# The first half of kv in neighbouring PSUM places, and x of two pairs in separate PSUM tiles

## The chip, the cores and the metric

The kernel runs on one core of one Trainium2 chip. The metric is the device time of one execution in microseconds (us); for one kernel I quote the median of its runs, with lowest and highest. All runs in this document were in the fast state, with a granted TensorE clock between 0.998 and 1.0 in the profiled ones. "The trace" is the record of one profiled execution, and its times count from the start of that execution's span. In the lines of the profile PE is TensorE at its matmuls, PEld TensorE loading weights, DVE VectorE, ACT ScalarE and POOL GpSimd; "issue" is time in which an engine waited for nothing that the profile shows. The chain is the work that ended last, followed back from the end. PSUM is the memory into which the matmuls write; it comes in banks, and a tile is a buffer that the kernel asks for, here of one or two banks.

## The reference

Linear attention over 8 batches of 8 heads (576 positions, 64 wide), followed by a two-layer feed-forward net with exact GELU over all 4608 tokens:

```
q_s = softmax of q over the head's 64 entries
k_s = softmax of k over the 576 positions
kv  = einsum('bhsd,bhse->bhde', k_s, v)        # 64 x 64 a head
x   = einsum('bhsd,bhde->bhse', q_s, kv)       # -> 4608 x 512, heads side by side
h   = x @ w_in                                 # 512 -> 2048
out = gelu(h) @ w_out                          # 2048 -> 512
```

The output is fp32. The kernel multiplies in bf16.

## The kernel before

Heads are taken two at a time, so a batch has four pairs (hp 0 to 3). For each batch the kernel makes kv of the pairs on TensorE (`kv_mm`, in two halves of two pairs), divides by the softmax sum of k on VectorE (`kv_norm`, result `kvc` in bf16), makes x from q and kvc (`x_mm`), copies x out of PSUM (`x_evac`, on VectorE with "v" or ScalarE with "s"), and then runs the two large products (`h_phase`, `y_phase`) on 512 tokens. The parts that matter here, with cuts:

```python
def kv_mm(b, half):
    if "kv" not in st[b]:
        st[b]["kv"] = psum_a.tile([128, 2, 2, 256], FP32, tag="a2", name="kv")   # two banks
    ps = st[b]["kv"]
    for n in range(NS):
        for i in range(2):                      # pair 2*half + i; i chooses the bank
            for hh in range(2):
                ...
                nc.tensor.matmul(ps[c, i, half, 0:D + 1], ek[...], v_aug[...],
                                 start=(n == 0), stop=(n == NS - 1))

def kv_norm(b, h0, h1):
    ps = st[b]["kv"]
    nc.vector.reciprocal(rec[:, :, 0:m], ps[:, :, h0:h1, D])
    nc.vector.tensor_tensor(out=kvc[b]..., in0=ps[:, :, h0:h1, 0:D], in1=rec..., op=ALU.mult)

# batch 0
kv_mm(0, 0)
kv_norm(0, 0, 1)
warm_x()                                        # four matmuls on zeros, to fill the wait
kv_mm(0, 1)
kv_norm(0, 1, 2)
x_mm(0, 0)
...
# batch 1, in between the second product of batch 0
xx = psum_a.tile([128, 2, M], FP32, tag="a2", name="xx")       # one tile, two banks
st[1]["x2"], st[1]["x3"] = xx[:, 0], xx[:, 1]
x_mm(1, 1)                                      # x of pairs 2 and 3
x_evac(1, 2)                                    # VectorE
x_evac(1, 3, "s")                               # ACT
...
h_phase(1, ..., groups={0: 2})                  # the first two column groups take turns
```

The softmax here doesn't subtract the row's maximum and nothing guards it: scores larger than these inputs give would overflow.

## Time and profile before

| | before |
|---|---|
| median of the first 3 runs | 279.95 us (279.80 to 280.01) |
| span of the profiled run | 278.2 us |
| TensorE (PE) busy | 271.6 us, 98% |
| large matmuls: pace in a full stage | 64 in 13.81 us, 0.2158 us each |
| stop in batch 0, before the second half of kv | 0.40 us |
| step from the sixth to the seventh matmul of batch 1's first product | 0.392 us (0.216 elsewhere) |

The page's shares are averages; that TensorE is the bound follows from the chain, where it makes 95% of what ended last. The last two rows of the table are the two holes in TensorE's stream that the change aims at. The lines that carry them stand in the prediction below.

### The profile page before, as it was taken

The page shows a single profiled execution, that of the slowest core. Times are in us where ns is not written, and L with a number is a line of the kernel's source. Part 1 is how long each engine was busy: PE and PEld are TensorE (multiplying, and loading weights), DVE is VectorE, ACT ScalarE, POOL GpSimd, SP SyncE. Part 2 cuts the span into 40 slices and gives each one's busy share as a digit, 9 for nine tenths or more (in the row PEclk, how much of TensorE's full clock was granted, in tenths as well). Part 3 has the DMA queues.
Part 4 walks back from the last instruction along what each step waited for, and adds up shares of the span by engine and source line. Part 5 has one row for each costly group of instructions (what it writes and reads, how often), then busy time and mean ns, then how long its engine had stood idle before and what let it go on. Part 6 is the DMA issues. An engine that isn't in the chain of part 4 may idle for free.

```text
span 278.2 us, 4570 instructions
## 1 busy us (share of the span) xinstructions
PE 271.6 (98%) x1924; PEld 126.0 (45%) x1924; DVE 100.7 (36%) x151; ACT 158.5 (57%) x246; POOL 33.9 (12%) x25
## 2 busy tenths in 40 slices
PE   7799999999999999999999999999999999999994
PEld 3344454444444444444444444444444444444443
DVE  2876574309743540183008400651015200120012
ACT  4867666689377816791569246943683363126400
POOL 1630050002020220014000500050005000000000
PEclk9999999999999999999999999999999999999999
DMA  7999999963993149602981199117401500220033
GB/s 255 396 394 431 398 398 407 400 247 94 292 350 62 65 106 282 268 38 85 268 329 38 43 229 390 50 48 192 112 0 75 151 2 0 75 78 0 0 78 77
DMA packets 44980, 50.10 MB, mean 180 GB/s; under 512 B 20384, under 2 KB 29856, under 8 KB 44704
## 3 DMA queue, kind: packets, MB, share of 16 engines
q1 hardware_dynamic: 44560, 49.39, 53.1%
q10 hardware_dynamic: 400, 0.43, 0.5%
q8 instruction: 15, 0.25, 0.4%
q14 instruction: 5, 0.04, 0.1%
HBM read 36.70 MB, written 9.44 MB: 166 GB/s over the span
## 4 chain that ended last, share of the span: by engine, by line
PE 95%; DMA 2%; DVE 1%; POOL 1%; ACT 0%; issue 0%; POOLq 0%
PE ps L311 44%; PE ps L321 44%; PE kv L180 2%; DMA f<-in_q_dram 2%; PE ps L268 1%; PE ps L346 1%; POOL e L212 1%; PE pair L311 1%; PE ps L229 1%; ACT e L145 0%; DVE qsum L210 0%; PE ps L273 0%; DVE kvc L191 0%; PE tp L229 0%; PE ps L430 0%
## 5 line engine op out<-in xcount | busy, mean ns | idle before, releaser
L311 PE MATMUL ps<-xT,wi_bf 128*128 128x512 bf16 x568 | 124.9, 379 | 0.0
L321 PE MATMUL ps<-wo_bf,g 128*128 128x512 bf16 x560 | 124.2, 379 | 0.0
L316 ACT ACTIVATE g<-ps 128x512 bf16<-128x512 f32 x142 | 83.8, 598 | 66.9 <-PE ps L311 66.9
L311 PEld LDWEIGHTS <-wi_bf 128*128 128x128 bf16 x576 | 56.2, 98 | 68.1 <-issue 0.7
L321 PEld LDWEIGHTS <-g 128*128 128x128 bf16 x560 | 53.9, 98 | 64.3 <-issue 0.4
L329 DVE COPY y_sb<-ps 128x512 f32<-128x512 f32 x34 | 23.2, 686 | 81.0 <-PE ps L321 80.7
L212 POOL TENSOR_TENSOR e<-e,recq 128x2048 bf16<-128x2048 bf16 (+1 forms) x9 | 25.7, 2855 | 176.4 <-DVE recq L211 148.3
L162 DVE CAST v_aug<-f 128x576 bf16<-128x576 f32 x25 | 17.1, 745 | 47.5 <-DMA f<-in_v_dram 47.5
L210 DVE TENSOR_REDUCE qsum<-e 128x16 f32<-128x1024 bf16 (+1 forms) x13 | 21.0, 1619 | 14.4 <-ACT e L145 14.4
L294 ACT CAST xT<-ps 128x512 bf16<-128x512 f32 x18 | 9.8, 589 | 25.8 <-PE ps L268 16.3
L145 ACT ACTIVATE e<-f 128x512 bf16<-128x512 f32 (+1 forms) x42 | 20.5, 556 | 3.4 <-DMA f<-in_q_dram 3.3
L150 ACT ACTIVATE ek<-f 128x2304 bf16<-128x2304 f32 (+1 forms) x10 | 17.2, 1728 | 0.5 <-DMA f<-in_k_dram 0.4
L292 DVE CAST xT<-ps 128x512 bf16<-128x512 f32 x16 | 10.3, 686 | 17.0 <-PE ps L268 14.1
L79 ACT ACT_TABLE_LOAD x9 | 11.5, 1283 | 2.8 <-issue 2.6
L430 PE MATMUL ps<-zeros 128*128 128x512 f32 (+1 forms) x16 | 8.5, 680 | 1.5 <-DVE zeros L464 1.5
L145 ACT ACT_TABLE_LOAD x7 | 9.0, 1283 | 0.1
L397 DVE CAST wi_bf<-w 128x512 bf16<-128x512 f32 x12 | 7.2, 632 | 2.3 <-DMA w<-in_moe_w_in_dram 2.0
L180 PEld LDWEIGHTS <-ek 64*64 64x64 bf16 x576 | 6.4, 105 | 2.7 <-issue 1.1
L180 PE MATMUL kv<-v_aug,ek 64*64 64x65 bf16 x576 | 6.8, 193 | 0.4 <-DVE kvc L191 0.4
L212 DVE TENSOR_TENSOR e<-e,recq 128x1024 bf16<-128x1024 bf16 x4 | 6.4, 1594 | 0.1
L423 DVE CAST wo_bf<-w 128x2048 bf16<-128x2048 f32 (+1 forms) x4 | 4.4, 1094 | 3.9 <-DMA w<-in_moe_w_out_dram 3.8
L430 PEld LDWEIGHTS ps<-zeros 128*128 128x128 f32 x14 | 3.2, 239 | 5.3 <-issue 3.8
(40 smaller groups left out, 51.2 us busy)
## 6 DMA issues: line engine op xcount, KB each, us to landing
out_dram<-y_sb SPq DMA_DIRECT2D x32, 256.0 KB, 2.4
f<-in_k_dram SPq DMA_DIRECT2D x6, 1152.0 KB, 9.5
f<-in_v_dram SPq DMA_DIRECT2D x6, 1152.0 KB, 11.6
f<-in_q_dram SPq DMA_DIRECT2D x6, 1024.0 KB, 7.2
w<-in_moe_w_in_dram SPq DMA_DIRECT2D x6, 512.0 KB, 8.8
f<-in_v_dram SPq DMA_DIRECT2D x8, 288.0 KB, 6.8
f<-in_q_dram SPq DMA_DIRECT2D x4, 512.0 KB, 8.9
w<-in_moe_w_out_dram SPq DMA_DIRECT2D x2, 1024.0 KB, 12.2
```

The lines of the kernel that those rows point to most:

```text
L79: nc.scalar.activation(out=scr[:, 1:2], in_=scr[:, 0:1], func=func)
L145: nc.scalar.activation(out=dst[:, i], in_=src[:, u], func=AF.Exp)
L150: nc.scalar.activation(out=ek[b % 2][:, i:i + n], in_=st[b]["kf"][:, i:i + n].rearrange("p x (n d) -> p x n d", n=NS), func=AF.Exp,)
L162: eng.tensor_copy(out=o, in_=i)
L180: nc.tensor.matmul(ps[c, i, half, 0:D + 1], ek[b % 2][pr, hp, n, :], v_aug[b % 2][pr, hp, n, 0:D + 1], start=(n == 0), stop=(n == NS - 1),)
L210: nc.vector.reduce_sum(out=qsum, in_=eq[:, :, hs, :], axis=AX.X)
L212: eng.tensor_tensor(out=eq[:, :, hs, :], in0=eq[:, :, hs, :], in1=recq.unsqueeze(3).to_broadcast([128, J, w, D]), op=ALU.mult,)
L311: nc.tensor.matmul(ps, wi_bf[:, dm, t * 128:(t + 1) * 128], xT[:, dm, :], start=(dm == 0), stop=(dm == NDM - 1),)
L316: nc.scalar.activation(out=g[:, t, :], in_=ps, func=AF.Gelu)
L321: nc.tensor.matmul(ps, st[c]["g"][:, t, j * 128:(j + 1) * 128], wo_bf[:, t, :], start=(t == 0), stop=(t == NDF - 1),)
L329: nc.vector.tensor_copy(out=y_sb, in_=ps)
L430: nc.tensor.matmul(ps, z[:, 0:128], z, start=True, stop=True)
```

## The change

The intent of the first part, as I read the diff: put pairs 0 and 1 into the two neighbouring places in the middle (the end of one bank and the start of the other), pairs 2 and 3 into the outer ones, so that scaling the first half reads one run of PSUM and the second half can be written meanwhile. The intent of the second: x of batch 1's pairs 2 and 3 in two tiles, so that the two engines that copy them out have nothing in common.

```diff
+    place = [1, 2, 0, 3]
+    def kvc_of(b, hp):
+        return kvc[b][:, hp if b < 2 else place[hp], :]
...
-            st[b]["kv"] = psum_a.tile([128, 2, 2, 256], FP32, tag="a2", name="kv")
+            st[b]["kv"] = psum_a.tile([128, 4, 256], FP32, tag="a2", name="kv")
...
-                        ps[c, i, half, 0:D + 1], ek[b % 2][pr, hp, n, :],
+                        ps[c, place[hp], 0:D + 1], ek[b % 2][pr, hp, n, :],
...
+            src, dst, m = ps[:, 1:3] if half == 0 else ps[:, 0::3], kvc[b][:, 2 * half:2 * half + 2], 2
...
-    xx = psum_a.tile([128, 2, M], FP32, tag="a2", name="xx")
-    st[1]["x2"], st[1]["x3"] = xx[:, 0], xx[:, 1]
+    x_tile(1, 2, psum_a, "a")
+    st[1]["x3"] = psum_a.tile([128, 2, M], FP32, tag="a2", name="xx")[:, 0]
```

The rest of the diff makes `x_mm` and `kv_norm` follow the new places; in batches 2 to 7 both halves are scaled in one instruction, as before, and kvc now keeps the order of the places.

More of the change, by code (lines that the diff above doesn't have):

```diff
@@ L180, in kv_mm, with kv_norm @@
                     nc.tensor.matmul(
-                        ps[c, i, half, 0:D + 1], ek[b % 2][pr, hp, n, :],
+                        ps[c, place[hp], 0:D + 1], ek[b % 2][pr, hp, n, :],
                         v_aug[b % 2][pr, hp, n, 0:D + 1], start=(n == 0), stop=(n == NS - 1),
                     )
-    def kv_norm(b, h0, h1):
+    def kv_norm(b, half=None):
         ps = st[b]["kv"]
-        m = h1 - h0
-        rec = small.tile([128, 2, 2], FP32, tag="reck")
-        nc.vector.reciprocal(rec[:, :, 0:m], ps[:, :, h0:h1, D])
+        if half is None:
+            src, dst, m = ps, kvc[b], 4
+        else:
+            src, dst, m = ps[:, 1:3] if half == 0 else ps[:, 0::3], kvc[b][:, 2 * half:2 * half + 2], 2
+        rec = small.tile([128, 4], FP32, tag="reck")
+        nc.vector.reciprocal(rec[:, 0:m], src[:, :, D])
         nc.vector.tensor_tensor(
-            out=kvc[b].rearrange("p (h i) d -> p i h d", i=2)[:, :, h0:h1],
-            in0=ps[:, :, h0:h1, 0:D],
-            in1=rec[:, :, 0:m].unsqueeze(3).to_broadcast([128, 2, m, D]), op=ALU.mult,
+            out=dst, in0=src[:, :, 0:D],
+            in1=rec[:, 0:m].unsqueeze(2).to_broadcast([128, m, D]), op=ALU.mult,
         )
@@ L199, in kv_step @@
         kv_mm(b, 1)
-        kv_norm(b, 0, 2)
+        kv_norm(b)
     def norm_q(b, i=0, n=1, eng=None):
@@ L268, in x_mm @@
                         nc.tensor.matmul(
-                            ps[c, :], kvc[b][pr, hp, :], st[b]["qT"][pr, :, hp, :],
+                            ps[c, :], kvc_of(b, hp)[pr], st[b]["qT"][pr, :, hp, :],
                             start=True, stop=True,
@@ L273, in x_mm @@
                         nc.tensor.matmul(
-                            ps[c, bb * R:(bb + 1) * R], kvc[bb][pr, hp, :],
+                            ps[c, bb * R:(bb + 1) * R], kvc_of(bb, hp)[pr],
                             st[b]["qT"][pr, bb // 2, hp, bb % 2 * R:(bb % 2 + 1) * R],
@@ L488 @@
     kv_mm(0, 0)
-    kv_norm(0, 0, 1)
+    kv_norm(0, 0)
     warm_x()
     kv_mm(0, 1)
-    kv_norm(0, 1, 2)
+    kv_norm(0, 1)
     x_mm(0, 0)
@@ L549 @@
     kv_mm(1, 0)
-    kv_norm(1, 0, 1)
+    kv_norm(1, 0)
     y_part(14, range(J))
@@ L557 @@
     x_evac(1, 1, "s")
-    kv_norm(1, 1, 2)
+    kv_norm(1, 1)
     y_part(15, range(J))
```

## The prediction

> **What bounds the kernel now.** I read the page first: engine shares, the 40 slices, the chain; then the chain in order of time around the two places that the diff touches (the start, batch 0, and the turn from batch 0 to batch 1), then the timeline of each engine there, then the groups by tile.
>
> ```profile
> PE 271.6 (98%) x1924; PEld 126.0 (45%) x1924; DVE 100.7 (36%) x151; ACT 158.5 (57%) x246; POOL 33.9 (12%) x25
> PE   7799999999999999999999999999999999999994
> PE 95%; DMA 2%; DVE 1%; POOL 1%; ACT 0%; issue 0%; POOLq 0%
> ```
>
> TensorE is busy in every slice, and 95% of the chain that ends last is its own work. So only what shortens TensorE's stream, or a hole in it, can move the end. Busy alone does not prove a full pace, so I checked the pace: the chain gives each full stage of the first product as 64 matmuls in 13.81 us, 0.2158 us each. The second product with its 560 and 32 matmuls (the last 32 are narrower) is at the same pace. The holes are what is left to win. The chain in order of time shows the two places:
>
> ```profile
> 12.48 0.30 DVE kvc L191
> 12.78 0.04 issue
> 12.82 0.52 PE kv L180 x35
> ```
>
> ```profile
> 44.25 0.34 PE xx L268 x4
> 44.59 1.40 PE ps L311 x6
> 45.99 0.01 issue
> 46.00 12.68 PE ps L311 x58
> ```
>
> In the first, at batch 0, TensorE stops before the second half of kv until VectorE has scaled the first half into kvc. In the second, at the start of batch 1's first product, 58 matmuls take 12.68 us, where 58 x 0.2158 = 12.52 us would do: 0.16 us is a stop before the seventh matmul. Starts of single matmuls in that trace say the same: 0.392 us between the sixth and the seventh, where 0.216 is usual, so 0.176 us lost. Between there and the tail I find no other interval of the big matmuls that is out of line; the switches to and from the 64-wide ones cost about 0.31 us each time, in every batch, and stay. What the seventh waits for is in the timeline of ACT and DVE:
>
> ```profile
> 44.64 0.69 DVE L292 CAST xT<-xx 128x512 bf16<-128x512 f32 x1 [0.20 <-PE xx L268]
> 45.37 0.59 ACT L294 CAST xT<-xx 128x512 bf16<-128x512 f32 x1 [0.82 <-DVE xT L292]
> ```
>
> The two tiles xx holds (x of pairs 2 and 3) lie in two banks and are copied out by two engines, yet ACT starts only when DVE has ended, after 0.82 us of idling. With two column groups at a time (the first group of this stage is a pair), matmuls one to six need pairs 0, 1 and 2, the seventh needs pair 3. Pair 3 is there at 45.37 + 0.586 = 45.96 and the seventh starts at 46.00.
>
> **What the Trainium skill says.** "Perfetto Trace Analysis", section "Optimization Strategy", tells to find the gaps between slices of the bounding engine and the semaphore that each waits for; that is the reading above. "TensorE: Matmul & The Clock Gate", section "Back-to-back issue gap", gives 216 ns for an isolated matmul of 512 columns (and a lower sustained figure, 131 ns, which this trace does not reach); the trace has 215.8. "PSUM — Partial Sum Buffer", section "PSUM bank collisions raise a hardware error", says that a write by TensorE and a read by another engine in one bank and quadrant collide whatever the addresses, and to guard by bank and quadrant, not by address. The trace agrees as far as it can: kv's second half waits 0.40 us for the read of the first half, at other addresses of the same banks. "VectorE: DVE Perf Modes", section "The TRN2 errata — SBUF-src ops pay a fixed extra latency per instruction", has (N+151)/0.96 ns for a fp32 tensor_tensor: 291 ns at 128 and 424 at 256. The trace has 291 for kvc at 128 and 424 to 426 at 256, in spite of its PSUM input[...].
>
> **The change part by part.** I compared the built programs: every engine has the same instructions in the same order; what differs is access patterns and a handful of waits.
>
> (1) *kv in neighbouring places.* Pairs 0 and 1 go from places 0 and 2 of 4 to places 1 and 2; pairs 2 and 3 to 0 and 3. The banks stay: places 0 and 1 are one bank, 2 and 3 the other. The aim can only be that the second half no longer falls within the span that the scaling of the first half reads, so that TensorE need not stop at 12.4 to 12.8 us. But in the changed program the first matmul of the second half has the same wait on VectorE as before, for the same count (13, the end of the scaling of the first half): the dependence is kept by bank, not by range. Removed: nothing. Of batch 1 the same: its second half comes behind x of the first half, which needs kvc anyway. Cost 0.
>
> (2) *kvc's order for batches 2 to 7.* Six scalings of 128x256 at 424 ns keep their 256 elements; by the formula above and the 424 to 426 ns of the trace they cost the same. They lie beside TensorE (DVE is 36% busy), and their result is used a stage later. Cost 0. x's matmuls read another 64-column block of kvc: same shape, 400 ns modelled, same count.
>
> (3) *x of pairs 2 and 3 in two tiles.* Pair 2 goes to the single bank "a" that held pair 0, pair 3 to the first bank of the two that held kv. The first matmul of pair 2 now waits for ACT to have emptied pair 0. That copy and the next were one 1.07 us run of ACT from 42.99, so it is done by about 43.6; x begins at 44.18. Slack 0.6 us, cost 0. The ACT copy of pair 3 now waits for TensorE (the last of the four matmuls) in place of VectorE. VectorE started on the same event at 44.64, and ACT's earlier work (y_sb, 43.95 + 0.60) ends at 44.55, so the copy starts at about 44.65 and ends at about 45.24, 0.72 us sooner. The seventh matmul, unhindered, would start at 46.00 - 0.176 = 45.83: 0.59 us after that. So the whole 0.176 us goes, and no more, since then TensorE's own pace is the limit. The fifth matmul needs pair 2: VectorE ends at 44.64 + 0.69 = 45.33 and, with 0.05 us from end to start as seen for ACT (45.96 to 46.00), allows 45.38; it started at 45.40. This doesn't change, but has just 0.02 us of slack.
>
> Two waits are added on ACT before later table loads, on VectorE's counts 10 and 37. Those were passed tens of us earlier. Cost 0.
>
> Sum: 0 + 0 - 0.176 us. All later work is one unbroken TensorE stream, so the gain is carried to the end: 279.95 - 0.18 = 279.77 us, 0.06%.
>
> **The rivals.** First: the kv wait goes after all. Then the second half could start about 0.4 us sooner (VectorE's rec and kvc, 12.27 to 12.78, would run beside it; some of it is hidden by warm_x, four matmuls put there to fill it). For: it is the purpose of the change, and the idle of 0.40 us is on the chain. Against: the wait is still in the program. It would give at best 279.35, probably less, as the casts of the first weights on GpSimd run from 13.20 to 16.28 us just ahead of TensorE, and would stop it instead.
>
> Second: the gain at batch 1 turns into another wait. With ACT and DVE reading PSUM at once, DVE's copy of pair 2 could be slower, and its slack is only 0.02 us; the fifth matmul would stop instead of the seventh. Against: in batch 0 the same two copies overlap and take 0.59 on ACT and 1.32 / 2 = 0.66 us on DVE, no more than alone. It would make the time 279.8 to 279.95.
>
> Third: the gain is swallowed downstream, by a transfer or a buffer that TensorE then meets 0.18 us early. For: transfers are dense until about 60 us. Against: no big matmul of the later stages starts late in the trace before, and waits of VectorE and GpSimd for transfers don't reach TensorE. It would make 279.95.
>
> Fourth: slower, by a worse access pattern of kv in PSUM. Against: places are still 256 words apart, runs of 65 columns are the same, and kv is 6.8 us of busy time in all, overlapped four by four. I see nothing over 0.1 us there.
>
> **Range and chances.** The three runs before lie within 0.21 us, so noise of a median is about 0.1 us and as large as the gain. The main line gives 279.77; the second and third rival up to 279.95, the first down to 279.35. With noise, 279.5 to 280.0 should hold 8 of 10. 2% would be 5.6 us. No part touches more than 0.6 us of TensorE's stream, so within 2% is all but certain.
>
> **What would show it.** Right: ACT's copy of pair 3 starts at about 44.65 beside DVE's; the chain shows the 64 matmuls of batch 1's first product without a break, 13.9 us in place of 14.09; TensorE's idle of 0.4 us before kv, put down to DVE kvc, is still there; every later stage stands about 0.18 us earlier with its own length, 13.81, kept. Wrong: no wait of kv for kvc in batch 0 (then the program's wait was not the one I took it for); a stop before the fifth matmul; a later stage that is longer than 13.81; VectorE's scalings off 424 ns. A different state of the chip or another clock than 0.999 would make the number wrong without touching the argument.

## More of the kernel before

The scheduling layer under the kernel adds the semaphore waits. The kernel only says which tile an instruction reads and writes.

## The result, and the profile after

| | runs | median | lowest to highest |
|---|---|---|---|
| before | 6 | 279.98 us | 279.80 to 280.07 |
| changed | 6 | 279.88 us | 279.76 to 280.19 |

All outputs are right. The ratio is 0.9999, with a 95% interval of 0.9986 to 1.0012. Ratios here are the mean time of one kernel's fast runs over that of the other's fast runs of the same rounds, so they are not quite the ratio of the medians. The whole time doesn't tell the two kernels apart: the expected gain of 0.06% is smaller than the interval's half width of 0.13%.

The trace can tell. First the same three lines of the page, now for the changed kernel. Its source lines are 8 to 11 higher, as the diff adds lines (the first product goes from L311 to L321, the second from L321 to L331).

```profile
PE 269.5 (97%) x1896; PEld 126.1 (45%) x1924; DVE 100.5 (36%) x151; ACT 158.4 (57%) x246; POOL 33.6 (12%) x25
PE   7799999999999999999999999999999999999995
PE 94%; DMA 2%; issue 1%; DVE 1%; POOL 1%; ACT 0%; POOLq 0%
```

Two numbers look like a change and are none. PE has 1896 instructions where the kernel before has 1924, yet PEld still has 1924 weight loads: 28 matmul records are missing from this trace (the repeat of the same kernel below has all 1924). Twenty of them leave a step of 0.43 us (two times 0.216) between their neighbours, the other eight lie at or just behind the switches from the 64-wide to the large ones; the chain books a part of such a step as "issue" (0.05 us at the one in batch 1's first product). The page thus shows TensorE 1% less busy though it lost no time there.

Next, the chain in order of time at batch 0 (start, duration, what), for the changed kernel. It answers to the first pair of chain lines in the prediction:

```profile
12.73 0.18 DVE rec L201
12.91 0.02 issue
12.94 0.30 DVE kvc L202
13.24 0.04 issue
13.28 0.52 PE kv L188 x33
```

The second half of kv still starts 0.04 us after VectorE has scaled the first. The wait is there, and its length in the list of waits is 0.4 us, as before. Everything stands 0.46 us later than in the trace before, because q, the first load, landed that much later in this execution (4.83 us in place of 4.38 on the chain); no part of the change touches that load. It fits that the profiled run, at 280.19 us, was the slowest of the six; the other five have no trace.

Then the timeline of the two copies of batch 1's pairs 2 and 3:

```profile
45.09 0.69 DVE L302 CAST xT<-ps 128x512 bf16<-128x512 f32 x1 [0.20 <-PE xx L278]
45.12 0.59 ACT L304 CAST xT<-xx 128x512 bf16<-128x512 f32 x1
```

They start 0.03 us apart; in the kernel before, ACT idled for 0.82 us and began when VectorE ended. For the chain through batch 1's first product I take the second trace of the changed kernel (the repeat below), as it lost no record there:

```profile
44.60 13.92 PE ps L321 x64
58.52 1.51 PE ps L331 x7
```

One unbroken row of 64 matmuls in 13.92 us stands where the kernel before had 1.40, a break, and 12.68. The end of that stage comes 0.17 us sooner after its start.

Since the load at the beginning varies by tenths of a microsecond, I compare stretches inside the traces that don't contain it. They are worked out from the start times of instructions, which a trace has to the nanosecond. Stretch A runs from batch 0's first kv matmul to the first matmul of its first product. Stretch B runs from the first matmul of batch 1's first product to the start of VectorE's last copy of the output.

| trace | A, us | step before the late matmul of batch 1, us | B, us |
|---|---|---|---|
| before | 2.526 | 0.392, the seventh | 230.186 |
| changed | 2.521 | none | 230.014 |
| changed, repeat | 2.522 | none | 230.023 |
| x tiles alone | 2.525 | none | 230.021 |
| kv places alone | 2.524 | 0.392, the seventh | 230.193 |
| copies turned round | 2.526 | 0.824, the fifth | 230.626 |
| kv in banks of its own | 2.332 | none | 230.022 |
| the same, repeat | 2.447 | none | 230.024 |

Without the reversed copies, B falls into two groups that agree within 0.01 us, and the change is worth 0.17 us of it. A doesn't move with the change. The piece between A and B takes 30.27 to 30.31 us in these traces (30.40 with the x tiles alone, see there), so over the whole way from batch 0's kv to the last copy the changed kernel gains 0.18 us in one trace and 0.13 in the repeat.

### The profile page after: what moved, and what is told of

Same layout as the page of the kernel before. It is cut to its first block, busy times and chain, and to the rows that moved or that the text cites. A ratio compares the mean times of both kernels' runs of the same rounds, so it can differ in the third digit from the quotient of the medians.

```text
span 278.4 us, 4542 instructions
## 1 busy us (share of the span) xinstructions
PE 269.5 (97%) x1896; PEld 126.1 (45%) x1924; DVE 100.5 (36%) x151; ACT 158.4 (57%) x246; POOL 33.6 (12%) x25
## 4 chain that ended last, share of the span: by engine, by line
PE 94%; DMA 2%; issue 1%; DVE 1%; POOL 1%; ACT 0%; POOLq 0%
PE ps L321 44%; PE ps L331 43%; PE kv L188 2%; DMA f<-in_q_dram 2%; PE ps L278 2%; PE ps L356 1%; POOL e L222 1%; PE pair L321 1%; PE ps L239 1%; ACT e L145 0%; DVE qsum L220 0%; PE ps L283 0%; DVE kvc L202 0%; PE tp L239 0%; PE ps L440 0%
## 5 line engine op out<-in xcount | busy, mean ns | idle before, releaser
L321 PE MATMUL ps<-xT,wi_bf 128*128 128x512 bf16 x557 | 124.2, 379 | 0.6
L331 PE MATMUL ps<-wo_bf,g 128*128 128x512 bf16 x543 | 122.1, 379 | 1.6 <-issue 1.1
L321 PEld LDWEIGHTS <-wi_bf 128*128 128x128 bf16 x576 | 56.2, 98 | 67.9 <-issue 0.2
L331 PEld LDWEIGHTS <-g 128*128 128x128 bf16 x560 | 53.9, 98 | 64.3 <-issue 0.4
L302 DVE CAST xT<-ps 128x512 bf16<-128x512 f32 x17 | 11.0, 686 | 17.1 <-PE ps L278 14.1
L278 PE MATMUL ps<-qT,kvc 64*64 64x512 bf16 x62 | 5.4, 389 | 0.4 <-DVE kvc L202 0.4
```

What stands on the lines that cost most here:

```text
L321: nc.tensor.matmul(ps, wi_bf[:, dm, t * 128:(t + 1) * 128], xT[:, dm, :], start=(dm == 0), stop=(dm == NDM - 1),)
L331: nc.tensor.matmul(ps, st[c]["g"][:, t, j * 128:(j + 1) * 128], wo_bf[:, t, :], start=(t == 0), stop=(t == NDF - 1),)
```

## The experiments

My theory: of the two parts only the separate tiles do anything, by letting ACT copy beside VectorE. One rival gives the gain to the kv places. Another says that the stop before the seventh matmul is not the copies' order at all. A third question was what the wait left at batch 0 would be worth.

**x tiles alone.** The kernel before, with this edit:

```diff
-    xx = psum_a.tile([128, 2, M], FP32, tag="a2", name="xx")
-    st[1]["x2"], st[1]["x3"] = xx[:, 0], xx[:, 1]
+    x_tile(1, 2, psum_a, "a")
+    st[1]["x3"] = psum_a.tile([128, 2, M], FP32, tag="a2", name="xx")[:, 0]
```

> The kernel before, with only x of batch 1's last two pairs in separate tiles. My theory (this part alone carries the gain): same waits in the built program as the full change, so ACT's copy of pair 3 starts within 0.1 us of VectorE's copy of pair 2, no 0.39 us step before the seventh matmul of batch 1's first product, and the stretch from the first kv matmul of batch 0 to the last instruction is 0.17 to 0.18 us shorter than in the kernel before; time 0.1 to 0.2 us less, within noise. Rival (the kv placing carries it): nothing changes, the step of 0.39 us is there.

Measured: 279.80 us (279.66 to 280.00, 5 runs) beside 280.01 of the kernel before (279.82 to 280.31, 9 runs); ratio 0.9992, interval 0.9978 to 1.0006. The step is gone and B is 230.021, as in the full change. The timeline of the two copies in this run:

```profile
44.66 0.69 DVE L292 CAST xT<-ps 128x512 bf16<-128x512 f32 x1 [0.20 <-PE xx L268]
44.70 0.59 ACT L294 CAST xT<-xx 128x512 bf16<-128x512 f32 x1
```

The expectation for the stretch from batch 0's kv to the end was missed, though: it came out 0.03 us shorter, not 0.17. In between, ahead of B, this execution lost 0.13 us: a matmul of batch 0's second product waited for ACT's cast of a row of w_out, which ended at 41.56 us. That lies before the copies of this part, at a place where the built program is the same, so I take it for variation of when the weights land.

**kv places alone.** The changed kernel with the shared xx tile put back (the edit above, reversed).

> The kernel before, with only the new places of kv; pairs 2 and 3 of x still share one tile. As the prediction put it (this part removes nothing): the 0.40 us idle before batch 0's second kv half stays, and the step of 0.39 us before the seventh matmul stays, time as before. Rival, from the built program: in it ACT's copy of pair 3 waits for TensorE and not for VectorE, even with the shared tile, so the step is gone here too, and the stretch from batch 0's kv to the end is 0.17 to 0.18 us shorter, as in the run with the tiles alone; then the two parts are two ways to take away one wait.

Measured: 279.92 us (279.83 to 280.00, 5 runs), ratio 0.9996, interval 0.9983 to 1.0008. Nothing has moved: A is 2.524, the step of 0.392 is there, B is 230.193. The timeline of the two copies in this run:

```profile
44.71 0.69 DVE L302 CAST xT<-xx 128x512 bf16<-128x512 f32 x1 [0.20 <-PE xx L278]
45.43 0.58 ACT L304 CAST xT<-xx 128x512 bf16<-128x512 f32 x1 [0.82 <-DVE xT L302]
```

So the theory holds and the rival falls. The premise of that rival was an error of mine: I had listed the built programs of several kernels and read the difference of the next experiment's program as this one's. This kernel's program has the very waits of the kernel before, and the trace shows the 0.82 us of idling that follows from them.

**Copies turned round.** The kernel before, with the copies in the other order, so that a dependence of one on the other would bite on the other side:

```diff
-    x_evac(1, 2)
     x_evac(1, 3, "s")
+    x_evac(1, 2)
```

> The kernel before, with the order of the two copies turned round in the program (pair 3 by ACT first, then pair 2 by VectorE). If the one-after-the-other of the two copies is the whole cause and TensorE meets it directly: ACT copies at once (ends about 0.65 us after the last of x's matmuls starts to be read), VectorE 0.04 us after that for 0.69 us, and now the fifth matmul waits in place of the seventh, for about 0.60 us, so 0.43 us slower than the kernel before and 0.6 slower than the changed one. Rival (the stop before the seventh matmul comes from something else, such as two engines reading PSUM or weight loads): the stop stays before the seventh, about 0.18 us, and the time as before.

Measured: 280.46 us (280.27 to 280.73, 5 runs), ratio 1.0016, interval 1.0003 to 1.0028: slower than the kernel before by 0.45 us in the median, clear of noise though under 2%. The chain in order of time says why:

```profile
44.27 0.37 PE xx L268 x4
44.64 0.02 issue
44.66 0.59 ACT xT L294
45.26 0.02 issue
45.28 0.70 DVE xT L292
45.98 0.04 issue
46.02 10.74 PE ps L311 x49
```

Now both copies are on the chain, one after the other, and the fifth matmul (the first to need pair 2) waits for the second of them. Its step is 0.824 us, 0.61 more than 0.216; 0.60 was expected. B is 0.44 us longer than before (expected 0.43). That settles what stops TensorE: whichever copy stands second in the program waits for the first, while both read one tile, in different banks. (In the runs without the wait both pairs lie in other banks than before, as well as in two tiles.) TensorE stops for as long as the late copy overruns the moment at which its data is needed.

**kv in banks of its own.** What would the wait at batch 0 be worth, had the change removed it? I did not simply leave it out, as TensorE would then write banks that VectorE is reading; no run tried that. In this kernel, the changed one otherwise, batch 0's second half goes to two tiles, each with a bank of its own (shortened, the comments are mine):

```diff
+        if b == 0 and half == 1:
+            own = [psum_h.tile([128, M], FP32, tag="h", name="kv") for _ in range(2)]
...
-                        ps[c, place[hp], 0:D + 1], ek[...]
+                        own[i][c, 0:D + 1] if b == 0 and half == 1 else ps[c, place[hp], 0:D + 1], ek[...]
...
+            for i in range(2):                       # kv_norm: one bank at a time
+                nc.vector.reciprocal(rec[:, 0:1], own[:, D:D + 1])
+                nc.vector.tensor_tensor(out=kvc[b][:, 2 + i], in0=own[:, 0:D], in1=rec..., op=ALU.mult)
...
     kv_mm(0, 1)
+    x_tile(0, 3, psum_h, "h")                        # was taken ahead of kv_mm(0, 0)
     kv_norm(0, 1)
```

> The changed kernel, with batch 0's second kv half in two banks of its own, so that it needs no wait for VectorE at all; VectorE scales it in two pairs of instructions in place of one. If the wait of 0.40 us was worth its length: 0.25 us or more gained over the changed kernel. My theory: the 0.40 us idle before the second kv half is gone, x of pairs 0 and 1 starts about 0.3 us sooner, but the first product starts only 0.2 to 0.25 us sooner because VectorE now has 0.25 us more scaling to do, and part of that is lost again to the weights that GpSimd is still casting (up to 0.25 us of stop before the eleventh matmul of the first product); net 0 to 0.2 us.

Measured: 279.55 us (279.50 to 279.63, 5 runs), ratio 0.9983 to the kernel before, interval 0.9970 to 0.9995: the first version whose gain is clear of noise, though it too is under 2%. The chain at batch 0:

```profile
11.82 0.41 PE kv L191 x36
12.23 0.22 PE ps L461 x4
12.45 0.50 PE kv L191 x36
12.94 0.16 DVE rec L202
13.10 0.02 issue
13.12 0.23 DVE kvc L203
13.36 0.04 issue
13.40 0.74 PE ps L291 x4
```

TensorE goes from the first half over the four filling matmuls (L461) into the second half without waiting for VectorE. It is not free of waits there, which the chain, counting the half as one piece, doesn't show; the timeline does:

```profile
10.22 2.14 POOL L162 CAST v_aug<-f 128x576 bf16<-128x576 f32 x2 [0.24 <-DMA f<-in_v_dram]
12.42 0.36 PEld L191 LDWEIGHTS <-ek 64*64 64x64 bf16 x33 [0.24 <-issue]
```

The third matmul of the half, the first that needs the fourth part of v, starts 0.139 us after the second (0.003 or 0.004 in the other kernels) and 0.053 us after GpSimd's cast of that part ended, at 12.36. A is 0.19 us shorter than in the changed kernel, just under the 0.2 to 0.25 expected for the start of the first product; from batch 0's kv to the end it gains 0.17 us, within the 0 to 0.2 expected. The stop for weights that GpSimd is still casting, which I had allowed for, did not come: the first product goes on at its usual pace.

**The change and that kernel again**, beside each other on another chip:

> The changed kernel once more, beside the next one on the same chip. If its gain is the one stop and nothing else: 0.1 to 0.2 us less than the kernel before (ratio 0.9993 to 0.9997), with an interval that still reaches 1. If something else grew by as much: ratio 1.000.

> The changed kernel with batch 0's second kv half in banks of its own, once more beside the changed kernel. If the wait that the change left in is worth 0.17 us, as its trace had it: 0.15 to 0.2 us less than the changed kernel and 0.3 to 0.45 less than the one before. If the first measurement was luck: same as the changed kernel.

Measured, with 9 runs of the kernel before at 279.92 us (279.81 to 280.42): the change 279.90 us (279.81 to 280.07, 5 runs), ratio 0.9998, interval 0.9986 to 1.0011; kv in its own banks 279.57 us (279.43 to 279.96, 5 runs), ratio 0.9987, interval 0.9973 to 1.0000. The change's time again can't be told from that of before; its ratio lies between the two that were expected (0.9993 to 0.9997, or 1.000). The banked kernel's gain is at the edge of the noise, and A is only 0.075 us shorter than in the change this time. Its chain shows what came in between:

```profile
11.79 0.05 issue
11.85 0.68 POOL v_aug L162
12.52 0.04 issue
12.56 0.53 PE kv L191 x34
13.09 0.16 DVE rec L202
```

GpSimd's cast of v's fourth part ends at 12.52, and the second half of kv needs it: its third matmul starts 0.258 us after the second, 0.12 more than in the first trace of this kernel, which is about the difference between the two A's. In the kernel before that cast ends at 12.47 and is hidden behind the wait for VectorE, which ends at 12.78. With the first wait gone, the second one is next, in both traces. Counted from the first kv matmul, that cast ended after 0.62 and 0.74 us in the two traces of the banked kernel and after 0.53 to 0.94 us in the other six, so what the separate banks gain can differ from execution to execution. By the traces the banked kernel gains 0.17 and 0.11 us over the change from batch 0's kv to the end; by the medians of the second session 0.33 us (0.15 to 0.2 was expected). The intervals of the times, some 0.35 us to each side, hold both; which is nearer stays open.

## Why the prediction was right

*What bounds the kernel.* Right: a hole in TensorE's stream that closed shortened the time from there to the end by just its length, 0.172 and 0.163 us in B for the two traces of the change, against 0.176 predicted. The third rival, a gain swallowed downstream, falls with it: in the repeat every later stage of the first product keeps its 13.81 us.

*Part 1, the places of kv: nothing removed.* Right, and no luck, as the wait was read off the built program. It stayed with its 0.40 us before the second half, and the places alone left A and B as they were. The fourth rival, a worse access pattern of kv, falls too, as A is 2.52 us in all of these. The aim of this part was missed. The reason that the prediction gives, a dependence kept "by bank, not by range", is not shown, though: the change leaves something of either half in each bank, but also all of it in one tile, and the experiment that removes the wait gives the second half tiles and banks of its own at once. The copies of xx, which wait in different banks of one tile, speak for the tile.

*Part 2, kvc's order: no cost.* Right. The six scalings of batches 2 to 7 took 424 to 425 ns, against 424 to 426 before.

*Part 3, the separate tiles: the whole gain.* Right in cause and size. The copy of pair 3 starts 0.03 us after that of pair 2, the seventh matmul doesn't stop, and the first product takes 13.92 us (13.9 predicted). The copies turned round show that the order of the two is the cause. The second rival, two engines reading PSUM at once and hindering each other, falls: 691 and 587 ns side by side, 692 and 586 one after the other. (The prediction's 0.66 us for VectorE in batch 0 is half the span of two copies; singly they took 0.68 and 0.69.) The fifth matmul, with its slack of 0.02 us, didn't stop.

*The sum.* The time of 279.88 us lies in the range, 0.11 above the 279.77 of the main line. But the prediction's own remark decides how much that proves: noise is as large as the gain, so the two sessions' medians, 0.10 and 0.02 us less than before, could not have shown a wrong step. The stretch B can, as it leaves out the start, and there the step stands.

*Side remarks that were wrong.* The first rival held that a kernel without the kv wait would then stop for GpSimd's casts of the first weights. It doesn't. What stands next behind that wait are the cast of v's fourth part and VectorE's scaling of the second half, in both traces; they leave 0.19 and 0.08 us of the 0.40. And the 0.31 us for a switch to the 64-wide matmuls are the whole step, 0.09 us more than the usual 0.216.

## What to carry to other kernels

A wait that a scheduling layer inserts follows the unit in which it keeps track, not the addresses: here, moving data within one tile and its banks removed nothing, and a tile with a bank of its own did (no run separates the two). Before taking a wait away, compute when the data is really needed and what else ends just before it: 0.72 us of ACT's delay were worth 0.17, and 0.40 us of TensorE's own wait 0.19 and 0.08 in the two traces. A gain under the noise of whole runs can still be shown, by a stretch inside the trace that leaves out the noisy start, and by an experiment that makes the suspected cost larger.

## What the Trainium skill lacked or had wrong

- "TensorE: Matmul & The Clock Gate", section "Back-to-back issue gap": it gives a sustained 131 ns for a matmul of 512 columns in a stream with weight loads, and calls the 216 ns formula an over-count there. Here such a stream, each matmul with its own weight load, runs at 215.8 ns in every full stage from batch 2 on (64 in 13.81 us), at a granted clock of 0.999.
- "VectorE: DVE Perf Modes", section "The TRN2 errata — SBUF-src ops pay a fixed extra latency per instruction": its row for PSUM sources, 120 + N cycles at 0.96 GHz (the row's speed factor taken as 1), would give 192, 258 and 392 ns for 64, 128 and 256 elements. tensor_tensor from PSUM took 224, 291 and 424 ns, which is the page's other formula, (N + 151) / 0.96, that it states for fp32 without naming PSUM.
- No page that I found gives the time from the end of one engine's copy to the start of the instruction on another engine that waits for it. Here it is 0.034 us from VectorE to ACT (45.334 to 45.368 us in the kernel before) and 0.050 us from ACT to TensorE (45.954 to 46.004).
